# Theta's weights cast on their way in, angles rounded to int32, and v of batch 1 held behind them

## The chip, the cores and the metric

The kernel runs on one core of one Trainium2 chip. The metric is the device time of one execution in microseconds; before the change its median over three runs is 208.49 us (208.44 to 208.51). The engines are called PE (TensorE), DVE (VectorE), ACT (ScalarE), POOL (GpSimd) and SP (SyncE, which here only issues transfers). Transfers are issued by SP and ACT (hardware queues, q1 and q10 in the profile) and by POOL (the software queue, q0), and all of them are carried by the same 16 DMA engines. Only transfers issued on POOL change the type on the way.

## The reference

q, k and v have 8 batches, 8 heads, 576 positions of 64 numbers. First comes a linear attention without a softmax, with its rows normalised; then a block that mixes tokens with a phase.

```
kv  = einsum('bhsd,bhse->bhde', k, v)
out = einsum('bhsd,bhde->bhse', q, kv)
x   = out / sqrt(mean(out*out, -1) + 1e-6) * g_norm        # then heads side by side: [8, 576, 512]
theta = x @ w_theta                                        # [512, 512]
y   = w_tok_r @ (x * cos(theta)) + w_tok_i @ (x * sin(theta))   # per batch, [576, 576]
u   = x + y
result = u + relu(u @ w_ch)                                # w_ch [512, 512]
```

## The kernel before

A batch is worked as 576 = 4 x 128 + 64 rows: four full row tiles (j = 0 to 3) and a tail of 64 rows (names that end in e). For each of the 8 batches TensorE forms k'v, turns q, multiplies it with k'v (raw), and the rows are normalised: ACT squares, DVE sums, a root (ACT for batch 0, POOL for the others), DVE scales to x in fp16. x is turned (by TensorE for the first four batches, by a transposing transfer later), scaled by g on ACT or DVE into xT, and multiplied with theta's weights `wth` (task th, line 451). The angle is then brought into one turn: ACT takes the whole turns (pt, line 467), DVE subtracts them (ar, line 472), an absolute value for the cosine (ab), ACT evaluates sine and cosine (lines 490 and 497), and DVE multiplies x with both (z). TensorE mixes tokens (y, line 543) with the turned token weights wT, DVE makes u, TensorE multiplies with `wch` (v in the trace's line 451), and DVE finishes.

How whole turns are taken: theta's weights are scaled by 1/TURN as they are cast to fp16, TURN being an eighth of a turn, so that the product comes in eighths; adding `MAGIC`, 1.5 * 2^23 * 8, in fp32 leaves only whole multiples of 8 eighths; DVE subtracts MAGIC again and then the angle, which leaves minus the rest.

Theta's weights come in on SP's queue as fp32, into memory that z of batch 1 uses later (`wth_s`, the tile zm1 in the trace), and four instructions scale and cast them (`scale_theta`, lines 241 and 245: three on ACT and one on DVE). z of batch 1 therefore depends on these four.

The order of the work is a list written out by hand: the program makes tasks with their dependencies, numbered as they are made, and `TURNS` names the numbers in the order in which they are issued (a star picks the second of two engines, r9 issues nine idle products). Each engine works its own instructions in that order and waits on semaphores for the others; nothing is reordered on the chip.

Three places of the start matter here. POOL's queue first issues q of batch 0, then a copy of one number of v's tails of batch 0 ("hold p", line 232), which waits until that transfer has landed; behind it stand the two token weights (w_tok_i, then w_tok_r: wn for 512 rows, wnt for the last 64), then a copy of one number of v of batch 1 ("hold v"), and behind that q of batches 1 and 2 and the channel weights. SP issues k of batch 0 and v's tails, g, theta's weights, v of batch 1 and k of batch 1, then k and v of later batches, whose buffers have to come free first. ACT's queue issues v's heads of batch 0. TensorE turns the token weights as tasks wt (lines 639 and 640), the first two of them between the first and the second theta product.

Of the kernel before, what the change touches and what calls it, by code (L numbers as in the profile page):

```python
# [9 lines left out]
FP32 = mybir.dt.float32  # L10
# [22 lines left out]
3 4 0 1 2 5 6 7 9 8 32 33 44 r1 52 38 18 19 20 21 22 11 10 13 25 26 23 24 27 29 210 31 30 45* 60 61*  # L33
34 35 39 40 41 36* 37 42* 43* 76 46 77* 53* 47 48 62 78 54 68 28 63 12 64 79 49 69 80 50 65 66 55
15* 16* r9 51 67 70 14 56 17* 71 87 85 88 102 57 81 86* 72 73 103 138 142 139 143 82 83 74 58 59 75
95 93 94* 96 89 90* 130 91 104 92* 97 109 123 84 106 105 131* 98 134 140 116 135* 99 141* 107 124
125 108 132 100 117 110 133* 101 111 118 112 146 136 127 126* 137 172 176 144 164 213 214 215 216
113 128 114 147 120 119* 121 145 129 115 122 177 165 219 220* 217 218 173 233 166 226 221 222 234*
168 178 235 174 167 357 206 208 207 209 223 175 179 391 236 224 237 392 169 148 160 170 156 240 227
377 149 157 225 171 228 241* 238 229 239 158 159 230 150 152 247 242 161 378 248 243 254 153 154 190  # L40
162 255 244 231 245 264 256 265 191* 155 151 163 232 384 192 266 246 249 257 385 197 370 258 271 193
371* 259* 180 181* 278 260 185 250 268 267* 269 272 251 252 364 365 366 367 279 273 280 281 270 261*
253 186 282 274* 285 187 262 275 276 286 195 368* 369* 372 386 287 188 263 292 200 202 373 361 212
211 362 363 512 359 360 358 194 532 521 515 516 517 518 374 375 387 196 293 201 277 294 388 198 283
288* 376 284 203 389 295* 296 289 519 297 182 379 390 327 315 407 393 328 380 520 199 543 508 509
510 511 290 183 408 381 319 320 316 405 394 298 291 422 398 317 321 329 395 382 396 383 406 423 399
318 322 330 397 307 400 303 401 402 415 424 403 416 417 522 308 523 404 524 525 411 409 410 323 309
310 299 533 413 534 419 418 425* 426 427 420 414 304 412* 535 536 300 324 305 306 526 311 312 325
# [51 lines left out]
def kernel(  # L100
# [24 lines left out]

    eps = 1e-6

    UNIT = 8.0
    MAGIC = 1.5 * 2.0 ** 23 * UNIT
    TURN = 2.0 * math.pi / UNIT  # L130
    SHRINK = 1.0 - 1e-6
# [765 lines left out]
    with tc.manual_schedule():  # L897
# [7 lines left out]
        for i in range(NKV):  # L905
            clear_tails(i)
# [31 lines left out]
```

## Time and profile before

| what | value |
|---|---|
| median of the runs | 208.49 us |
| the profiled execution, its span | 208.02 us, 206.0 us |
| TensorE, VectorE, ScalarE, GpSimd busy | 187.4, 172.7, 138.9, 85.8 us |
| granted TensorE clock | 1.000 |
| DMA engines | 43.67 MB, mean 212 GB/s |
| casts of theta's weights on ACT and DVE | 3 x 619 ns, 1 x 417 ns |
| whole turns on ACT, 512 columns | 32 x 596 ns |
| subtraction on DVE, 512 columns | 32 x 681 ns |

Times inside the profile count from the span's start. The span is from the first to the last instruction; the execution's own time is 2.0 us longer. A row of a timeline gives start, duration, engine, line, instruction and, in brackets, the idle time of the engine just before it and what ended it. A row of a transfer gives size and the time from its issue to its landing. The page shows the DMA engines busy by nine tenths or more in all but one of the first 32 of 40 slices, so transfers stand in each other's way over most of the run.

### The profile page before, as it was taken

Reading aid. Unit: us, or ns where it says so; the run is one execution under the profiler, and the core shown is the slowest. Engines: PE = TensorE matmul, PEld = TensorE weight load, DVE = VectorE, ACT = ScalarE, POOL = GpSimd, SP = SyncE. Lnnn points to the kernel's source line nnn. Section 1 sums busy time; section 2 is a strip of 40 time slices with the busy share of each in tenths; the row PEclk is TensorE's granted clock in tenths of the full one; section 3 lists DMA queues with packets and bytes.
Section 4 is the critical chain, followed back from the end, with each engine's and each line's share of the span. In section 5 each row is a group of like instructions: output and inputs, shape, how many; then the busy total and the mean of one; then the engine's idle time right before and its main releaser. Section 6 shows DMA issues by size and latency. Waiting matters only on the chain.

```text
span 206.0 us, 5268 instructions
## 1 busy us (share of the span) xinstructions
PE 187.4 (91%) x2078; PEld 132.3 (64%) x2078; DVE 172.7 (84%) x362; ACT 138.9 (67%) x275; POOL 85.8 (42%) x90
## 2 busy tenths in 40 slices
PE   0378799999999999999999999997989999999992
PEld 0355468895786777576776767665856746756671
DVE  6039896789999999999898999996989999689572
ACT  2018799758799588987896678666936983976101
POOL 7030061263965565884608381283629420101300
PEclk9999999999999999999999999999999999999999
DMA  6999999999999899999999999999999552644144
GB/s 197 269 269 303 231 244 189 276 354 265 231 178 186 243 277 212 293 261 170 223 233 190 302 231 130 225 219 309 282 158 238 132 101 79 179 127 153 45 123 153
DMA packets 74952, 43.67 MB, mean 212 GB/s; under 512 B 44577, under 2 KB 70497, under 8 KB 74929
## 3 DMA queue, kind: packets, MB, share of 16 engines
q1 hardware_dynamic: 59216, 33.17, 67.7%
q0 software_dynamic: 14512, 9.00, 28.6%
q10 hardware_dynamic: 1200, 1.18, 1.7%
q8 instruction: 16, 0.26, 0.5%
q14 instruction: 8, 0.06, 0.1%
HBM read 33.06 MB, written 9.44 MB: 206 GB/s over the span
## 4 chain that ended last, share of the span: by engine, by line
PE 59%; DMA 15%; ACT 11%; DVE 10%; issue 2%; SPq 1%; DVEq 0%; POOL 0%; ACTq 0%
PE y L543 28%; PE th L451 10%; PE v L451 9%; DMA vt<-in_v_dram 5%; DMA wnt<-in_moe_w_tok_i_dram 4%; DMA qD<-qh 4%; DVE arg L472 2%; PE raw L323 2%; DMA uD<-wn 2%; ACT kbd L286 2%; ACT sc L497 2%; ACT sc L490 1%; DVE zm L520 1%; ACT arg L480 1%; PE wps L639 1%
## 5 line engine op out<-in xcount | busy, mean ns | idle before, releaser
L364 POOL TENSOR_TENSOR rt<-ss,mhalf 128x8 f32<-128x8 f32 (+1 forms) x35 | 54.6, 1563 | 66.3 <-DVE ss L354 66.0
L543 PE MATMUL y<-wT,zm 128*128 128x320 f16 (+1 forms) x512 | 76.8, 286 | 0.8 <-DVE ot L585 0.6
L543 PEld LDWEIGHTS <-zm 128*128 128x128 f16 x512 | 48.1, 98 | 15.8 <-issue 1.3
L548 DVE SCALAR_TENSOR_TENSOR wn<-y,gcol,xT 128x320 f16<-128x320 f32 (+1 forms) x64 | 30.9, 510 | 6.6 <-PE y L543 6.3
L451 PE MATMUL th<-wth,xT 128*128 128x512 f16 x128 | 32.1, 379 | 1.3 <-ACT xT L419 1.0
L467 ACT ACTIVATE arg<-th 128x512 f32<-128x512 f32 (+1 forms) x40 | 21.8, 554 | 14.4 <-PE th L451 13.9
L451 PE MATMUL v<-wch,wn 128*128 128x512 f16 x124 | 30.7, 380 | 0.0
L266 PE MATMUL kv<-vt,kt 128*64 128x64 f32 x640 | 21.6, 228 | 8.6 <-DMA vt<-in_v_dram 8.6
L345 ACT ACTIVATE sqb<-raw 128x512 f32<-128x512 f32 x32 | 18.8, 594 | 14.5 <-PE raw L323 14.5
L497 ACT ACTIVATE sc<-arg,quarter 128x512 f16<-128x512 f32 (+1 forms) x40 | 26.6, 675 | 0.3
L266 PEld LDWEIGHTS kv<-vt,kt 128*64 128x64 f32 x640 | 20.6, 143 | 9.5 <-issue 9.2
L472 DVE SCALAR_TENSOR_TENSOR arg<-arg,th 128x512 f32<-128x512 f32 (+1 forms) x40 | 24.9, 628 | 1.9 <-ACT arg L467 1.5
L490 ACT ACTIVATE sc<-arg 128x512 f16<-128x512 f32 (+1 forms) x40 | 22.7, 583 | 3.2 <-DVE arg L472 2.7
L354 DVE TENSOR_REDUCE ss<-sqb 128x8 f32<-128x520 f32 x32 | 22.0, 687 | 3.3 <-ACT sqb L345 3.3
L520 DVE TENSOR_TENSOR zm<-x,sc 128x1024 f16<-128x1024 f16 x32 | 21.8, 685 | 1.8 <-ACT sc L497 1.5
L386 DVE TENSOR_TENSOR x<-raw,rt 128x512 f16<-128x512 f32 x32 | 21.7, 684 | 0.8 <-POOL rt L364 0.5
L451 PEld LDWEIGHTS <-xT 128*128 128x128 f16 x128 | 11.6, 98 | 11.4 <-ACT xT L419 1.4
L451 PEld LDWEIGHTS <-wn 128*128 128x128 f16 x124 | 11.5, 98 | 10.7 <-issue 0.4
L480 ACT ACTIVATE arg<-arg 128x512 f32<-128x512 f32 (+1 forms) x31 | 17.5, 575 | 1.2 <-DVE arg L472 1.1
L543 PE MATMUL y<-wT,zt 128*128 128x320 f16 (+1 forms) x64 | 18.3, 286 | 0.0
L286 ACT CAST kbd<-kv 64x256 f16<-64x256 f32 (+1 forms) x24 | 8.5, 355 | 12.9 <-PE kv L266 12.6
L286 ACT COPY us<-ups 128x512 f16<-128x512 f16 (+1 forms) x17 | 8.5, 497 | 12.6 <-PE ups L281 11.5
(82 smaller groups left out, 229.7 us busy)
## 6 DMA issues: line engine op xcount, KB each, us to landing
vt<-in_v_dram SPq DMA_DIRECT2D x7, 1024.0 KB, 10.1
kt<-in_k_dram SPq DMA_DIRECT2D x7, 1024.0 KB, 8.2
out_dram<-ot SPq DMA_DIRECT2D x24, 256.0 KB, 2.7
qh<-in_q_dram POOLq DMA_DIRECT2D x7, 512.0 KB, 8.0
out_dram<-ot POOLq DMA_DIRECT2D x7, 256.0 KB, 3.6
kt<-in_k_dram SPq DMA_DIRECT2D x2, 512.0 KB, 4.6
vt<-in_v_dram ACTq DMA_DIRECT2D x2, 512.0 KB, 8.5
kt<-in_k_dram SPq DMA_DIRECT2D x8, 128.0 KB, 7.8
```

What stands on the lines that cost most here:

```text
L266: nc.tensor.matmul(t[i * D:(i + 1) * D, hp - lo, :], ks, vs, start=(hp == lo and j == 0), stop=(hp == lo + n - 1 and j == NT - 1),)
L354: nc.vector.reduce_sum(out=ss[:], in_=sq_sb.pop((b, j))[:], axis=AXX)
L364: nc.gpsimd.tensor_tensor(out=rt[:], in0=ss[:], in1=mhalf[:, 0:h], op=ALU.pow)
L386: nc.vector.tensor_tensor(out=x_pair[b, p][:, :, a * HC:(a + 1) * HC].rearrange("p t (h e) -> p h t e", e=D), in0=r[:].rearrange("p (h t e ...
L451: nc.tensor.matmul(t[:], piece(kc), w[:, kc, :], start=first, stop=last)
L467: nc.scalar.activation(out=arg[:, 1, :], in_=th_ps[b, j][:], func=AFT.Copy, bias=MAGIC)
L472: nc.vector.scalar_tensor_tensor(out=arg[:, 0, :], in0=arg[:, 1, :], scalar=MAGIC, in1=th_ps.pop((b, j))[:], op0=ALU.subtract, op1=ALU.sub ...
L490: nc.scalar.activation(out=sc[:, 0, :], in_=arg_sb[b, j][:, 0, :], func=AFT.Sin, bias=0.0, scale=-TURN * SHRINK,)
L497: nc.scalar.activation(out=sc_sb[b, j][:, 1, :], in_=arg_sb.pop((b, j))[:, 1, :], func=AFT.Sin, bias=quarter[:], scale=-TURN * SHRINK,)
L520: nc.vector.tensor_tensor(out=dst, in0=x.unsqueeze(1).broadcast_to((P, 2, w)), in1=sc[:], op=ALU.mult)
L543: nc.tensor.matmul(t[:, 0:hi - lo], s, wT[:, w, lo:hi], start=n == 0, stop=n == len(z) - 1)
L548: nc.vector.scalar_tensor_tensor(out=uTb[b % NUT][:, c, lo:hi], in0=y_ps.pop((b, h, c))[:, 0:hi - lo], scalar=gcol[:, 0:1], in1=xTb[b % NX ...
```

## The change

Five edits go together.

- Theta's weights are issued on POOL's queue and land in `wth` as fp16, unscaled. The four scalings and `wth_s` are gone, and z of batch 1 no longer waits for them.
- The whole turns are made by ACT as the angle times 1/TURN, TURN now being a whole turn, written as int32, the conversion rounding to a whole number. DVE reads the angle from PSUM, multiplies it with 1/TURN and subtracts that int32. The rest has the other sign than before, and so has the scale of the sine.
- A new task "hold w" on POOL adds one number of v's buffer of batch 1 and one of `wth`. It waits until theta's weights have landed.
- The load of v of batch 1 waits for "hold w" (it writes the number that "hold w" reads). So it starts only after theta has landed.
- One number of that buffer is set to zero by DVE at the start, so that "hold w" reads something defined.

In `TURNS` the four scalings, the old load of theta and the new tasks shift all numbers by three; apart from the removed and the added tasks the order is the same. The load of theta stands behind q of batch 0, "hold w" behind the token weights.

```
     def theta_in():
-        nc.sync.dma_start(out=wth_s, in_=moe_w_theta.rearrange("(kc p) c -> p kc c", p=P))
+        nc.gpsimd.dma_start(out=wth[:], in_=moe_w_theta.rearrange("(kc p) c -> p kc c", p=P))
...
+    def hold_both(a, b):
+        nc.gpsimd.tensor_tensor(out=gate[:], in0=a, in1=b, op=ALU.add)
...
-    def scale_theta(kc, eng):
-        if eng == "ACT":
-            nc.scalar.activation(
-                out=wth[:, kc, :], in_=wth_s[:, kc, :], func=AFT.Copy, scale=1.0 / TURN
-            )
-        else:
-            nc.vector.tensor_scalar(
-                out=wth[:, kc, :], in0=wth_s[:, kc, :], scalar1=1.0 / TURN, scalar2=None,
-                op0=ALU.mult,
-            )
...
     def whole_turns(b, j):
...
-        nc.scalar.activation(out=arg[:, 1, :], in_=th_ps[b, j][:], func=AFT.Copy, bias=MAGIC)
+        nc.scalar.activation(
+            out=arg[:, 1, :].bitcast(I32), in_=th_ps[b, j][:], func=AFT.Copy, scale=1.0 / TURN
+        )
...
     def reduce_arg(b, j):
         nc.vector.scalar_tensor_tensor(
-            out=arg[:, 0, :], in0=arg[:, 1, :], scalar=MAGIC,
-            in1=th_ps.pop((b, j))[:], op0=ALU.subtract, op1=ALU.subtract,
+            out=arg[:, 0, :], in0=th_ps.pop((b, j))[:], scalar=1.0 / TURN,
+            in1=arg[:, 1, :].bitcast(I32), op0=ALU.mult, op1=ALU.subtract,
         )
...
-            bias=0.0, scale=-TURN * SHRINK,
+            bias=0.0, scale=TURN * SHRINK,
...
-    wth_in = add("load wth", "SP", theta_in)
-    got["wth"] = [add(f"wg {kc}", "DVE|ACT", lambda e, kc=kc: scale_theta(kc, e), [wth_in])
-                  for kc in range(NKC)]
+    got["wth"] = [add("load wth", "POOL", theta_in)]
...
+    ahead = add("hold w", "POOL", lambda: hold_both(vt[1][0:1, 0:1], wth[0:1, 0, 0:1]), got["wth"])
...
-                       lambda t=t, src=src: heads_in(nc.sync, t, src, b, all8), old),
+                       lambda t=t, src=src: heads_in(nc.sync, t, src, b, all8),
+                       [*old, *([ahead] if t is vt[1] and b == 1 else [])]),
...
-                    [co, *of("y", b - NZ), *(got["wth"] if b == 1 else [])],
+                    [co, *of("y", b - NZ)],
...
+        nc.vector.memset(vt[1][0:1, 0:1], 0.0)
```

The first place where the order shows it is POOL's queue at the start (wth is theta's weights, wn and wnt the token weights, vt_66 and vt_67 v of batches 0 and 1, qh and qe the rows and tails of q; in brackets the semaphores waited for). Before:

```order
L209 DMA qe_71<-in_q_dram 64x4x64 x2
L232 COPY gate<-vt_66 1x1 [waits DMAHW5_49]
L215 DMA wn_86<-in_moe_w_tok_i_dram 128x2304
L220 DMA wnt_88<-in_moe_w_tok_i_dram 64x576
L215 DMA wn_85<-in_moe_w_tok_r_dram 128x2304
L220 DMA wnt_87<-in_moe_w_tok_r_dram 64x576
L232 COPY gate<-vt_67 1x1 [waits DMAHW1_49,Pool_49]
L203 DMA qh_69<-in_q_dram 128x8x256 [waits DMASW0_49]
```

and now:

```order
L206 DMA qe_71<-in_q_dram 64x4x64 x2
L220 DMA wth<-in_moe_w_theta_dram 128x4x512
L232 COPY gate<-vt_66 1x1 [waits DMAHW5_49]
L212 DMA wn_86<-in_moe_w_tok_i_dram 128x2304
L217 DMA wnt_88<-in_moe_w_tok_i_dram 64x576
L212 DMA wn_85<-in_moe_w_tok_r_dram 128x2304
L217 DMA wnt_87<-in_moe_w_tok_r_dram 64x576 [waits DMASW0_49]
L229 TENSOR_TENSOR gate<-vt_67,wth 1x1 [waits DMASW4_49,DVE_49,Pool_49]
L232 COPY gate<-vt_67 1x1 [waits DMAHW0_49,Pool_49]
L200 DMA qh_69<-in_q_dram 128x8x256 [waits DMASW1_49]
```

Theta's load stands ahead of the first gate and of the token weights, and the new gate stands behind the token weights and ahead of the old gate on v of batch 1.

The second place is SP's queue at the start (kt is k, gcol is g, zm_77 the memory in which theta's weights landed). Before:

```order
L193 DMA vt_66<-in_v_dram 64x8x64
L229 DMA gcol<-in_g_norm_dram 64x1 x2
L223 DMA zm_77<-in_moe_w_theta_dram 128x4x512 [waits DMAHW0_49]
L187 DMA vt_67<-in_v_dram 128x8x256 [waits DMAHW1_49]
L193 DMA vt_67<-in_v_dram 64x8x64 [waits DMAHW2_49]
L187 DMA kt_65<-in_k_dram 128x8x256 [waits DMAHW3_49]
```

and now:

```order
L190 DMA vt_66<-in_v_dram 64x8x64
L226 DMA gcol<-in_g_norm_dram 64x1 x2
L184 DMA vt_67<-in_v_dram 128x8x256 [waits DMAHW0_49,Pool_49]
L190 DMA vt_67<-in_v_dram 64x8x64 [waits DMAHW1_49]
L184 DMA kt_65<-in_k_dram 128x8x256 [waits DMAHW2_49]
```

Theta's load is gone from SP, and the load of v of batch 1, with its tails and k of batch 1 behind it, waits for POOL's gate.

The third place is ScalarE's part of batch 0 (sqb the squares, wth<-zm the scalings, xT the scaled turned x, rs the roots, arg the whole turns). Before:

```order
L345 ACTIVATE sqb_94<-raw 128x8x64
L241 ACTIVATE wth<-zm_77 128x512 x3
L345 ACTIVATE sqb_95<-raw 128x8x64
L419 ACTIVATE xT_82<-xps,gcol 128x4x128
L373 ACTIVATE rs<-ss 128x8
```

and now:

```order
L334 ACTIVATE sqb_94<-raw 128x8x64
L334 ACTIVATE sqb_95<-raw 128x8x64
L408 ACTIVATE xT_82<-xps,gcol 128x4x128
L362 ACTIVATE rs<-ss 128x8
L362 ACTIVATE rs<-ss 128x4
```

The three scalings between the two squares are gone; the rest of ScalarE's order is the same. On VectorE the one scaling goes likewise, behind the first two x.

More of the change, by code (lines that the diff above doesn't have):

```diff
@@ L126 @@
     eps = 1e-6
[L128 to L130 removed]
+    TURN = 2.0 * math.pi
     SHRINK = 1.0 - 1e-6
```

101 lines of the change are left out of this document (50 added, 51 removed).

## The prediction

> **What bounds the kernel now.** I read the page's totals first, then the chain of waits, then the first 37 us engine by engine, because every edit but one acts there.
>
> ```profile
> span 206.0 us, 5268 instructions
> PE 187.4 (91%) x2078; PEld 132.3 (64%) x2078; DVE 172.7 (84%) x362; ACT 138.9 (67%) x275; POOL 85.8 (42%) x90
> PE y L543 28%; PE th L451 10%; PE v L451 9%; DMA vt<-in_v_dram 5%; DMA wnt<-in_moe_w_tok_i_dram 4%; DMA qD<-qh 4%; DVE arg L472 2%; PE raw L323 2%; DMA uD<-wn 2%; ACT kbd L286 2%; ACT sc L497 2%; ACT sc L490 1%; DVE zm L520 1%; ACT arg L480 1%; PE wps L639 1%
> ```
>
> TensorE is busy 187.4 of 206.0 us, and the third row, the chain of waits by line, has most of its weight there too, with two transfers of the start behind it (v and the tail of w_tok_i). A change of the start is therefore worth what it moves TensorE's first full stretch, if no transfer is due in the meantime. The chain in order of time (start, duration, what), with TensorE's first products ahead of it:
>
> ```profile
> 8.57 1.98 PE L266 MATMUL kv<-vt,kt 128*64 128x64 f32 x32 [8.57 <-DMA vt<-in_v_dram]
> 2.59 10.96 DMA vt<-in_v_dram
> 14.27 8.78 DMA wnt<-in_moe_w_tok_i_dram
> 23.10 0.22 PE wps L640
> 23.81 0.97 PE th L451 x4
> ```
>
> TensorE's idle time is 18.6 us in all, and 8.57 of it are this first wait. The tails of v of batch 0 land at 13.55, POOL's gate opens, the token weights are issued, the tail of w_tok_i lands at 23.05, TensorE turns it and goes on to the second theta product. But a second path ends almost at the same place, and it is the one that the change touches. The timelines of TensorE and ScalarE (start, duration, instruction, idle before it and what ended it):
>
> ```profile
> 19.65 0.38 PE L323 MATMUL raw<-kbd,qT 128*128 128x128 f16 x4 [0.26 <-DVE x L386]
> 21.77 1.04 PE L451 MATMUL th<-wth,xT 128*128 128x512 f16 x4 [1.00 <-ACT xT L419]
> 23.75 1.04 PE L451 MATMUL th<-wth,xT 128*128 128x512 f16 x4
> 18.99 1.66 ACT L241 ACTIVATE wth<-zm 128x512 f16<-128x512 f32 x3
> 20.55 0.58 ACT L345 ACTIVATE sqb<-raw 128x512 f32<-128x512 f32 x1
> 21.02 0.69 ACT L419 ACTIVATE xT<-xps,gcol 128x512 f16<-128x512 f16 x1
> 24.82 0.60 ACT L467 ACTIVATE arg<-th 128x512 f32<-128x512 f32 x1 [0.29 <-PE th L451]
> 25.43 1.28 ACT L377 ACT_TABLE_LOAD   x1
> ```
>
> The first theta product waits 1.00 us for ScalarE's xT, which stands behind three scalings of theta's weights and a square. The second must be over before ScalarE's arg of 24.82 and the table load behind it.
>
> **The change, part by part.**
>
> *The scalings go.* ScalarE's three take 20.55 - 18.99 = 1.56 us of its queue. Not all of it comes back: the square behind them needs the raw product that TensorE ends at 20.03, so it starts at about 20.08 instead of 20.55, and xT at 20.57 instead of 21.02. The gain at the first theta product is 0.45 us (21.32). VectorE's one scaling frees room too:
>
> ```profile
> 20.11 0.42 DVE L245 TENSOR_SCALAR wth<-zm 128x512 f16<-128x512 f32 x1
> ```
>
> Behind it stands VectorE's xT for the second theta product, which moves up by as much as it can and was ahead of need before. The two theta products start 23.75 - 21.77 = 1.98 us apart, and between them stand two turns of w_tok_i, of which the first waits for the landing of 23.05, some 0.1 us. If w_tok_i is there by 22.2 (rows) and 22.5 (tail), the second product starts at 23.2 instead of 23.75: 0.55 us. From there all three engines run the same order as before, TensorE nearly without a gap, and the 0.55 us stand.
>
> *Theta's weights move from SP's queue to POOL's.* They are issued behind q of batch 0, about 4.5 instead of 4.82 us.
>
> ```profile
> 3.17 1.27 POOL L209 DMA_DIRECT2D qe<-in_q_dram  x2
> zm<-in_moe_w_theta_dram SPq DMA_DIRECT2D x1, 1024.0 KB, 11.9
> qe<-in_q_dram POOLq DMA_DIRECT2D x2, 32.0 KB, 11.4
> wn<-in_moe_w_tok_i_dram POOLq DMA_DIRECT2D x1, 576.0 KB, 8.7
> ```
>
> Before, theta lands at 4.82 + 11.9 = 16.7, and the second of q's two last parts near 15.7. Now theta follows q in the same queue. The nearest transfer of its kind is the channel weights, same shape and cast; in the stretch 37 to 38 us, when they are most of the queue's work, it moved 0.21 MB in 1 us, so 0.52 MB take 2.5 us. The queue of k and v is then empty, since v of batch 1 is held, so q should end near 14 to 15 and theta near 16.5 to 17.5. It is due at 21.3: the wait costs nothing.
>
> *The token weights stand behind theta.* They are issued at 13.7 as before. The views of the DMA queues (packets, MB, share of the 16 engines) for 0 to 14 and 14 to 17.2 us, then both queues for 18 to 24, then 37 to 38:
>
> ```profile
> q1 hardware_dynamic: 2426, 1.63, 46.2%
> q1 hardware_dynamic: 830, 1.20, 102.4%
> q0 software_dynamic: 315, 1.08, 89.7%
> q1 hardware_dynamic: 310, 0.32, 18.7%
> q0 software_dynamic: 229, 0.21, 127.7%
> ```
>
> In 14 to 17.2 k's and v's queue (q1) carries theta's rest and the head of v; w_tok_i then flows at 0.18 MB/us against v. Its 0.66 MB take 3.7 us at that pace, so starting at 16.5 to 17.5 it ends at 20.2 to 21.2, ahead of 22.5. w_tok_r follows, ahead of its old time. No loss.
>
> The Trainium skill, "DMA: Bandwidth & Descriptors", section "Queues, rings and completion order", says that an engine takes turns between queues packet by packet. The 315 against 310 packets agree. By that rule theta in POOL's queue could take turns with the tails of k and v, which it stood behind before, and push the landing of 13.55 out; only q in front of it prevents that.
>
> *v of batch 1 is held.* The gate "hold w" needs theta, and stands on POOL behind the four token issues.
>
> The rows of both queues stand with the change above: theta went in on POOL ahead of the first gate, a gate on theta ahead of the one on v, and on SP the load of v of batch 1 now waits for POOL. Behind it on SP stand v's tails and all of k of batch 1; the next on SP are k and v of later batches at 35.65, behind a wait for TensorE's products. On POOL stand "hold v", q of batches 1 and 2 and the channel weights. What they had:
>
> ```profile
> 6.51 1.82 SPq L187 DMA_DIRECT2D vt<-in_v_dram  x1
> vt<-in_v_dram SPq DMA_DIRECT2D x1, 1024.0 KB, 20.7
> 35.65 0.99 SPq L187 DMA_DIRECT2D kt<-in_k_dram  x2
> 27.77 1.97 POOL L203 DMA_DIRECT2D qh<-in_q_dram  x2
> qh<-in_q_dram POOLq DMA_DIRECT2D x1, 512.0 KB, 8.0
> 36.48 0.39 PE L281 MATMUL qps<-ident,qh 128*128 128x128 f16 x4
> vt<-in_v_dram SPq DMA_DIRECT2D x1, 128.0 KB, 8.2
> 52.38 0.74 PE L266 MATMUL kv<-vt,kt 128*64 128x64 f32 x17
> 55.18 1.04 PE L451 MATMUL th<-wth,xT 128*128 128x512 f16 x4 [0.25 <-DVE xT L421]
> ```
>
> v is issued at about 17 instead of 6.5, but its first bytes moved only once theta was through. Of the 1.20 MB in 14 to 17.2, theta's rest is about 0.73 (by 14 us q1 had moved 1.63 MB, 0.32 beyond k and the tails of v), so v loses a head start of about 0.47 MB, or 1.2 us of the engines. In return the token weights flow unopposed in that time, and leave v the engines 2 us earlier. The work is the same; if the engines stay busy, v lands near 27.2 again, and q of batch 1 at 27.77 + 8.0 = 35.8. TensorE asks for it at 36.48 - 0.55 = 35.93: just in time. The tails of v of batch 2 (this view's 8.2 us belong to the issue at 44.19) land at 52.4 and are needed eight products after 52.38, now after 51.83: a stall of 0.3 us, of which the 0.25 us that TensorE waited at 55.18 swallow nearly all.
>
> *The rounding.* ScalarE writes int32 with a scale instead of fp32 with a bias, VectorE reads PSUM first and int32 second, 40 times each.
>
> ```profile
> L472 DVE SCALAR_TENSOR_TENSOR arg<-arg,th 128x512 f32<-128x512 f32 x32 | 21.7, 681 | 1.9 <-ACT arg L467 1.5
> L585 DVE SCALAR_TENSOR_TENSOR ot<-v,us 128x512 f32<-128x512 f32 x15 | 10.2, 683 | 0.3
> L467 ACT ACTIVATE arg<-th 128x512 f32<-128x512 f32 x32 | 18.9, 596 | 14.4 <-PE th L451 13.9
> L497 ACT ACTIVATE sc<-arg,quarter 128x512 f16<-128x512 f32 x32 | 22.7, 718 | 0.3
> ```
>
> PSUM as first operand costs 683 against 681 ns. No row has an int32 conversion. Bounds: nothing below (no row of these forms is faster by more than noise), and above the 122 ns by which the dearest activation exceeds this one; VectorE's has 2% of the chain, some 4 us or six instructions, and ScalarE's fewer, so up to 1 us for both. I take 0, from the row of the same operation.
>
> **Sum:** -0.55 at the start, and 0.1 taken off for transfers that are due later and do not move: -0.45. The profiled execution took 208.02 us (206.0 and 2.0 around it), 0.47 under the median of 208.49; its sum is 207.57, and the same difference from the median gives **208.05 us**.
>
> **Rivals.**
>
> *The held v comes late (slower).* Place: "hold v" and the q behind it. If the token weights do not start until 17.5, as before, the engines idle for the 1.2 us that v had. v lands at 28.4, q of batch 1 at 37.0 against 35.93: 1.0 us of stall against 0.55 of gain; the v tails of batch 2 land at 53.6, 0.95 late on the old plan, of which 0.25 are swallowed. One stretch gives some of it back, 30 to 31 us, in which the transfers kept the 16 engines 0.68 busy (the last two numbers: DMA share, GB/s):
>
> ```profile
> 30.00:31.00 1.00, 1.00 (x12) 0.74 (x13) 1.00 (x4) 1.00 (x4) 1.00 (x3) 1.00 0.68 82
> ```
>
> That is 0.3 us. The end is 0.4 to 0.7 later: 209.0. It decides from a delay of v of about 0.6 us. For it: the token weights issued at 13.7 moved nothing up to 17. Against it: the queue ahead of them was then full, and now is not. The Trainium skill, "SBUF — State Buffer", section "SBUF: two separate sides", says that some VectorE operations keep GpSimd from writing the descriptors of its DMAs, and that SP's queue is free of this; by that rule the token weights, issued on POOL while VectorE works, could start late whatever stands ahead of them, which is this rival at 209.0; the trace shows the late start, not its cause.
>
> *The start gains, and it is gone later (no change).* q of batch 1, with 0.15 us to spare, or some later transfer holds TensorE on the old time: 208.4.
>
> *The conversion is dearer than the forms next to it (slower or same).* 0.5 us of the 1 against the gain: 208.55.
>
> *More than the start's 0.55.* If the raw product did not hold the square, 1.56 us would come back: 207.0. The 0.26 us of TensorE's own wait at 19.65 speaks against it.
>
> **How the numbers follow.** Forecast 0.44, late v 0.25, gone later 0.20, conversion 0.06, more 0.05. About 0.2% (0.42 us) is what a measurement tells from no change. The forecast's own range, 207.8 to 208.25, straddles it: 0.32 of its chance count as faster, 0.12 as the same. Of the late v 0.16 pass the bound and 0.09 do not, of the conversion half. Faster 0.32 + 0.05 = 0.37; slower 0.16 + 0.03 = 0.19; the same 0.12 + 0.09 + 0.20 + 0.03 = 0.44. The range reaches from 207.6 to 209.1, so that it takes in the price of the late v.
>
> **What would show it.** Right: no scaling rows; ScalarE's xT near 20.6, the first theta product near 21.3, the second near 23.2; w_tok_i's tail before 22.5; v of batch 1 at 27 to 27.5 and no wait for q at 36; L467's and L472's rows at 596 and 681 ns. Wrong: a wait of TensorE for wth or wnt in the twenties, for qh near 36 or for vt near 52, or VectorE's row above 700 ns.

## The result, and the profile after

The changed kernel takes 207.05 us (median of 7 runs, 206.56 to 207.78) against 208.49 us for the kernel before in the same series; the ratio is 0.9927, 95% interval 0.9906 to 0.9947. That is 1.44 us less, about three times the 0.45 forecast and below the forecast range. Two later series (e4 and e15 below) gave 0.9945 (0.9915 to 0.9976) and 0.9924 (0.9897 to 0.9951), or 1.19 and 1.41 us between the medians. Ratios and intervals leave out executions more than 1.5% above the fastest of the same kernel; medians and ranges are over all executions. The profiled execution took 206.56 us. Single executions of either kernel spread by a microsecond or more, so the terms below are read from profiles, stage by stage, and only their sum from times.

The page of the changed kernel, its first rows:

```profile
span 204.6 us, 5267 instructions
PE 188.3 (92%) x2078; PEld 132.8 (65%) x2078; DVE 172.5 (84%) x362; ACT 137.6 (67%) x272; POOL 86.4 (42%) x92
```

ScalarE has three instructions fewer, GpSimd two more. The timelines of TensorE and ScalarE at the start (start, duration, instruction, idle before it and what ended it), then GpSimd's gate for theta and the two landings that mattered (size, time from issue):

```profile
17.79 2.11 PE L640 MATMUL idle<-fill,ident 128*128 128x512 f16 x9
21.53 1.04 PE L440 MATMUL th<-wth,xT 128*128 128x512 f16 x4 [0.60 <-ACT xT L408]
22.73 0.22 PE L631 MATMUL wps<-ident,wnt 64*128 64x64 f16 x1
23.37 1.04 PE L440 MATMUL th<-wth,xT 128*128 128x512 f16 x4
20.30 0.60 ACT L334 ACTIVATE sqb<-raw 128x512 f32<-128x512 f32 x1 [1.04 <-PE raw L312]
20.80 0.68 ACT L408 ACTIVATE xT<-xps,gcol 128x512 f16<-128x512 f16 x1
17.02 0.18 POOL L229 TENSOR_TENSOR gate<-vt,wth 1x1 f32<-1x1 f32 x1 [0.78 <-DVE qT L277]
wnt<-in_moe_w_tok_i_dram POOLq DMA_DIRECT2D x1, 72.0 KB, 6.2
vt<-in_v_dram SPq DMA_DIRECT2D x1, 1024.0 KB, 9.8
```

ScalarE now waits for the raw product and works xT at once; TensorE waits 0.60 us for it instead of 1.00. Theta's gate is passed at 17.0, w_tok_i's tail needs 6.2 us instead of 8.8 and lands near 20.8, two microseconds before TensorE turns it; v of batch 1, issued at 17.2, lands at 27.0. The whole turns and their subtraction, from the groups of instructions of the changed kernel:

```profile
L456 ACT ACTIVATE arg<-th 128x512 int32<-128x512 f32 x32 | 18.9, 597 | 14.1 <-PE th L440 13.7
L463 DVE SCALAR_TENSOR_TENSOR arg<-th,arg 128x512 f32<-128x512 f32 x32 | 21.8, 685 | 1.9 <-ACT arg L456 1.5
```

That is 597 against 596 ns, and 685 against 681.

Set instruction against instruction, TensorE in the changed kernel is 0.37 us ahead of its old time from 23 us on and stays so to 139 us: no wait for q at 36, none for v's tails at 52. Then come two more steps. At 140 us the transposed q of batch 6 is waited for; this row of TensorE's timeline is from before, the next from after:

```profile
140.62 0.40 PE L323 MATMUL raw<-kbd,qD 128*128 128x128 f16 x4 [1.46 <-DMA qD<-qh]
```

```profile
139.70 0.40 PE L312 MATMUL raw<-kbd,qD 128*128 128x128 f16 x4 [0.89 <-DVE x L375]
```

The wait is 0.57 us shorter (in the second row q has landed and VectorE's x ends the wait), and nearly all of that stays to TensorE's end, 1.00 us ahead. And the span ends 1.4 us earlier: behind the last store, which ScalarE issues (rows of before and after), the old kernel has 206.0 - 202.5 = 3.5 us, the new one 204.6 - 201.5 = 3.1.

```profile
202.51 0.37 ACTq L613 DMA_DIRECT2D out_dram<-ot  x1
```

```profile
201.51 0.36 ACTq L604 DMA_DIRECT2D out_dram<-ot  x1
```

So in this pair the start gives 0.37, the wait at 140 us 0.6 and the end 0.4. Which of them belong to the change was the question.

### The profile page after: what moved, and what is told of

Its sections match the earlier page's. It is cut to its first block, busy times and chain, and to the rows that moved or that the text cites. A ratio compares the mean times of both kernels' runs of the same rounds, so it can differ in the third digit from the quotient of the medians.

```text
span 204.6 us, 5267 instructions
## 1 busy us (share of the span) xinstructions
PE 188.3 (92%) x2078; PEld 132.8 (65%) x2078; DVE 172.5 (84%) x362; ACT 137.6 (67%) x272; POOL 86.4 (42%) x92
## 4 chain that ended last, share of the span: by engine, by line
PE 67%; ACT 12%; DVE 8%; DMA 7%; issue 2%; POOL 1%; DVEq 0%; ACTq 0%; POOLq 0%
PE y L534 29%; PE th L440 11%; PE v L440 11%; DMA vt<-in_v_dram 5%; PE kv L255 3%; PE raw L312 3%; DMA uD<-wn 2%; DVE arg L463 2%; ACT kbd L275 2%; ACT sc L488 2%; PE wps L630 2%; ACT sc L481 1%; ACT arg L471 1%; ACT xT L408 1%; PE qps L270 1%
## 5 line engine op out<-in xcount | busy, mean ns | idle before, releaser
L456 ACT ACTIVATE arg<-th 128x512 int32<-128x512 f32 (+1 forms) x40 | 21.8, 554 | 14.1 <-PE th L440 13.7
L334 ACT ACTIVATE sqb<-raw 128x512 f32<-128x512 f32 x32 | 18.9, 595 | 14.4 <-PE raw L312 14.3
L488 ACT ACTIVATE sc<-arg,quarter 128x512 f16<-128x512 f32 (+1 forms) x40 | 26.6, 675 | 0.3
L463 DVE SCALAR_TENSOR_TENSOR arg<-th,arg 128x512 f32<-128x512 f32 (+1 forms) x40 | 25.0, 632 | 1.9 <-ACT arg L456 1.5
L471 ACT ACTIVATE arg<-arg 128x512 f32<-128x512 f32 (+1 forms) x31 | 17.5, 575 | 1.2 <-DVE arg L463 1.1
```

What stands on the lines that cost most here:

```text
L456: nc.scalar.activation(out=arg[:, 1, :].bitcast(I32), in_=th_ps[b, j][:], func=AFT.Copy, scale=1.0 / TURN)
L463: nc.vector.scalar_tensor_tensor(out=arg[:, 0, :], in0=th_ps.pop((b, j))[:], scalar=1.0 / TURN, in1=arg[:, 1, :].bitcast(I32), op0=ALU.mul ...
L488: nc.scalar.activation(out=sc_sb[b, j][:, 1, :], in_=arg_sb.pop((b, j))[:, 1, :], func=AFT.Sin, bias=quarter[:], scale=-TURN * SHRINK,)
```

## Experiments

**The rounding alone**, in the kernel before (e1), and **the scalings alone taken out** (e2).

```
 e1  -  ACT: arg = th + MAGIC (fp32)      +  ACT: arg = int32(th / 8)
     -  DVE: (arg - MAGIC) - th           +  DVE: th / 8 - arg
 e2      def scale_theta(kc, eng):
     +      return
     ...
     +  nc.vector.memset(wth[:], 0.0)
```

> The kernel before with the rounding alone: theta's weights still scaled by 8/(2*pi) after landing, ScalarE writes the whole turns as int32 with scale 1/8, VectorE multiplies PSUM by 1/8 and subtracts the int32. Everything else as before. Theory A (the rounding costs and saves nothing; it all comes from the start): 208.49 within 0.2 us; the 40 + 40 instructions keep their means of 596 and 681 ns; TensorE's instructions stand where they stood, no shift above 0.1 us, and the transposes of uD around 122 to 127 us again take some 5.1 us on SP. Theory B (the rounding feeds the later gain, for instance through VectorE reading SBUF second): TensorE's shift grows in steps along the batches and the time falls by 0.3 us or more. A second use: if SP's 2.5 us issue at 123 us is an accident of one profiled execution, it is gone here though nothing ahead of it moved.

> The kernel before without the four scalings: the weights that the theta product reads are set to zero once at the start and theta's own load goes on as before, on SP and into the same scratch, and is not used, so the angles come out as zero and the output is another one. Loads, queues and the hold are those of before; only the start of ScalarE and VectorE is relieved. Theory A (the start alone does it, and what comes later, at 122 to 140 us, follows from everything standing earlier): first theta product about 0.4 us earlier, the later gain at 140 us too, time 207.1 to 207.4. Theory B (the later gain belongs to the moved loads of the start): the first theta products 0.2 to 0.45 us earlier, that shift constant to the end, time 208.0 to 208.2. Theory C (the tail of w_tok_i, which lands at 23.05 with the old loads, holds the second theta product whatever ScalarE does): shift at most 0.1 us from 23 us on, time 208.4 to 208.5.

e1: 208.82 us, ratio 1.0015 (0.9989 to 1.0042). By the time the rounding costs between -0.2 and 0.9 us; its groups keep their times to within 3 ns per instruction:

```profile
L467 ACT ACTIVATE arg<-th 128x512 int32<-128x512 f32 x32 | 18.9, 596 | 14.3 <-PE th L451 13.9
L474 DVE SCALAR_TENSOR_TENSOR arg<-th,arg 128x512 f32<-128x512 f32 x32 | 21.8, 684 | 1.9 <-ACT arg L467 1.5
```

The wait at 140 us was 0.82 us here, with nothing changed ahead of it. Over the profiles that leave SP's order and TensorE's start alone it is 0.79 to 1.52 us with the old loads and 0.58 to 1.45 with the new: it varies from execution to execution, and the 0.57 us of the first pair are not shown to be a gain of the change.

e2: 209.22 us, ratio 1.002 (0.9986 to 1.0054). TensorE's timeline shows why nothing came of it:

```profile
17.56 2.10 PE L650 MATMUL idle<-fill,ident 128*128 128x512 f16 x9
23.32 0.22 PE L641 MATMUL wps<-ident,wnt 64*128 64x64 f16 x1 [0.24 <-DMA wnt<-in_moe_w_tok_i_dram]
23.97 1.04 PE L452 MATMUL th<-wth,xT 128*128 128x512 f16 x4
```

ScalarE is free, and w_tok_i's tail lands at 23.3: theory C. The nine idle products give a measure for the rest: they start 2.41 to 2.45 us behind the end of batch 0's k'v in every profile, however late k and v come, and the second theta product follows 6.41 us after their start here.

**The hold taken out** of the changed kernel (e3), **the scalings put back** into it (e7), and **the hold alone** in the kernel before (e9).

```
 e3  -  ahead = add("hold w", "POOL", lambda: hold_both(...), got["wth"])
     +  ahead = add("hold w", "POOL", lambda: None)
     -  nc.vector.memset(vt[1][0:1, 0:1], 0.0)
 e7  +  ACT x3, DVE x1:  wth[:, kc, :] = 1.0 * wth[:, kc, :]     (old places in TURNS)
 e9  +  POOL, behind the token weights:  gate = vt[1][0, 0] + wth_s[0, 0, 0]
     +  nc.vector.memset(vt[1][0:1, 0:1], 0.0)
     (load of v of batch 1 moved behind it)
```

> The changed kernel without the hold: v of batch 1 is issued on SP near 6.5 us as before and waits for nothing, the gate on theta is gone from GpSimd; theta still lands cast through GpSimd's queue, unscaled. Prediction's reading (v takes turns with the token weights, and w_tok_i lands late): w_tok_i's tail lands at 22.5 to 23.5 us, the second theta product 0.1 to 0.5 us later than with the hold, time 207.1 to 207.5. If the later gain at 140 us hangs on when v and q of batch 1 land: TensorE's shift against the kernel before stays at the start's -0.1 to -0.4 and does not grow at 140 us, time 208.1 to 208.4. If the hold is worth nothing: 207.0 within 0.15.

> The changed kernel with four scalings by 1.0 put back at their old places in the orders of ScalarE (three) and VectorE (one), in place on theta's weights; loads, hold and rounding stay changed. If the relief of ScalarE is what the start gains (the prediction's step): the first theta product 0.2 to 0.45 us later than in the changed kernel, near 21.75 to 22.0 us, the second near 23.7 to 23.9, time 207.4 to 207.8. If the moved loads are what the start gains, because w_tok_i no longer comes at 23 us or later: th second product within 0.1 us of 23.36, time as the changed kernel's. The end stays at 3.9 us either way.

> The kernel before with the hold alone: GpSimd's gate on theta's landing (theta still on SP, fp32, scaled) stands behind the four token issues, and v of batch 1 waits for it; scalings, rounding and the 113 DMAs of SP and ScalarE as before. If the moved loads are worth something only together with the relief of ScalarE (the reading so far: w_tok_i and ScalarE's queue end together): w_tok_i's tail lands at 20 to 22 us, the first theta product stays at its time behind the scalings, the end of the span stays 4.3 us behind the last product, time 208.2 to 208.7. If the hold by itself carries most of the gain: second theta product near 23.4 us and time at or below 207.9. If v of batch 1, held, comes late without the cast load: wait for q near 36 us, time above 208.8.

e3: 209.32 us, ratio 1.0008 (0.9976 to 1.0040). The row of the wait that came:

```profile
23.99 0.41 PE L630 MATMUL wps<-ident,wn 128*128 128x128 f16 x4 [1.34 <-DMA wn<-in_moe_w_tok_i_dram]
```

v of batch 1, issued early, runs beside w_tok_i, which takes 9.9 us; the second theta product comes 7.30 us after the idle products. The mechanism was expected, at less than a third of its size (0.1 to 0.5 us, against 7.30 - 5.58 = 1.7, of which the wait is about 1.5), and with a time of 207.1 to 207.5 us. Behind the wait comes something that was not expected, the second theta product at half the pace:

```profile
25.16 1.89 PE L440 MATMUL th<-wth,xT 128*128 128x512 f16 x4
```

It takes 1.89 us instead of 1.04. The granted clock is 0.50 for 3.41 us from 24.6 us on in this profile, and batch 1 comes another 1.1 us late (10.5 us behind this product instead of 9.4). Over e3's executions, the seven with a granted clock of 0.996 or more take 207.43 to 209.39 us (median 208.07), the five below it 209.34 to 214.25. So without the hold no gain is left in the time, but how much of that is the wait and how much the clock was not separated.

e7: 208.23 us, 0.9979 (0.9962 to 0.9996). e9: 209.17 us, 1.0013 (0.9982 to 1.0043). Both lie above the times expected (207.4 to 207.8, 208.2 to 208.7); of the gain e7 keeps 0.44 us, about as much as the end's term below. Their TensorE rows, e7 first:

```profile
18.14 2.11 PE L651 MATMUL idle<-fill,ident 128*128 128x512 f16 x9
22.29 1.04 PE L451 MATMUL th<-wth,xT 128*128 128x512 f16 x4 [1.00 <-ACT xT L419]
24.14 1.04 PE L451 MATMUL th<-wth,xT 128*128 128x512 f16 x4
```

```profile
17.83 2.11 PE L657 MATMUL idle<-fill,ident 128*128 128x512 f16 x9
22.09 1.04 PE L459 MATMUL th<-wth,xT 128*128 128x512 f16 x4 [1.01 <-ACT xT L427]
23.93 1.04 PE L459 MATMUL th<-wth,xT 128*128 128x512 f16 x4
```

In both w_tok_i is early (5.5 to 6.4 us from issue) and ScalarE's scalings hold the product with the old wait of 1.0 us. From the idle products to the second theta product it is 6.00 and 6.10 us. With the same measure the changed kernel has 23.37 - 17.79 = 5.58, and 5.58 to 5.59 in each of its other profiles with the hold; the kernel before has 5.99 in e1 and e6, and 23.75 - 17.29 = 6.46 in its own profile. The 0.40 us between 5.99 and 5.59 lie ahead of the first theta product: that is ScalarE's relief.

The further 0.47 us of the kernel before have two parts. Only 0.14 lie between the two theta products (1.98 us apart there; 1.84 in the changed kernel, e1 and e6), where w_tok_i is waited for. The other 0.33 come from q's tails of batch 0, which TensorE turns ahead of the raw products (before, then after):

```profile
15.85 0.27 PE L281 MATMUL qps<-ident,qe 128*128 128x128 f16 x2 [1.01 <-DVE kbd L288]
```

```profile
15.29 0.28 PE L270 MATMUL qps<-ident,qe 128*128 128x128 f16 x2
```

The second part of these tails lands at 15.71 before and at 14.54 after. (The row of before names VectorE for the wait; but there and in e2, e6, e9, e11 and e14 TensorE starts 0.13 to 0.14 us behind this landing.) With theta on SP it lands at 15.7 to 16.4 us, with theta on GpSimd and the hold at 14.4 to 14.7, with theta on GpSimd and no hold (e3) at 15.3. Where batch 0's k'v ends early (14.84 in before, 15.11 in e2), the late tails push VectorE's first x, and the raw product behind it, back by 0.33 us against the idle products (x starts 1.62 us after their start instead of 1.29); where it ends later, by 0.11 (e9) or not at all (e1, e6).

So ScalarE's relief is worth 0.40 us at the same start, and the moved loads up to 0.47 us on top when k'v ends early. Neither shows in a time without the other.

**The end's list.** At the end SP waits for eight semaphores, DMAHW0 to DMAHW7, which the transfers of SP and ScalarE take in turn. The moments at which SP passed these waits, from the trace (the first is another wait):

```
before  202.61 | 204.66 204.73 204.79 204.85 204.91 204.97 205.03 205.09
after   201.61 | 201.67 201.73 201.80 201.86 201.92 202.81 203.34 203.66
```

Before, the last store holds the first wait, and seven that are long fulfilled follow at 0.06 us each. After, it holds the last. The two queues issued 113 transfers before (113 = 14 x 8 + 1) and 112 after, because theta's moved to GpSimd. To test it, one late store changes its queue, in the changed kernel to SP (e5: 113), in the kernel before to GpSimd (e6: 112):

```
 e5  TURNS:  - 1043*   + 1043
 e6  TURNS:  - 1040    + 1040*
```

> The changed kernel with one late store (half of batch 6's second row block group, issued by GpSimd near 190 us) moved to SP's queue, which is idle there; nothing else. Theory L (the list of waits at the end): the program ends with SP waiting, one after another, for eight DMA semaphores that the DMAs of SP and ScalarE take in turn; before there were 113 of them and the last store had the first place in the list, so seven waits of 0.06 us stood behind its landing, after there were 112 and it has the last place. With 113 again the time from the start of TensorE's last product to the end of the span is 4.3 us instead of 3.9, and the time 0.4 us above the changed kernel's, in 207.4 to 208.1. Theory S (the shorter end belongs to the changed transfers or is scatter): that time stays at 3.9 us, and the kernel's time with it.

> The kernel before with one late store (batch 6, first rows, issued by SP near 190 us) moved to GpSimd's queue, so that SP and ScalarE issue 112 DMAs. Theory L (the list of waits at the end): the time from the start of TensorE's last product to the end of the span is 3.9 us instead of 4.3, and the time 0.4 us below the kernel before, ratio 0.998; nothing before 180 us moves. Theory S: 4.3 us, ratio 1.000.

The last store and the span of e5, then of e6:

```profile
202.50 0.37 ACTq L604 DMA_DIRECT2D out_dram<-ot  x1
span 206.0 us, 5267 instructions
```

```profile
203.11 0.36 ACTq L613 DMA_DIRECT2D out_dram<-ot  x1
span 206.2 us, 5268 instructions
```

3.5 us in e5 (the changed kernel with 113 transfers), 3.1 in e6 (the one before with 112): the end has swapped with the count, theory L. In time e6 is 0.50 us below the kernel before (0.9977, 0.9949 to 1.0005, an interval that still holds no change), e5 0.99 us below it (0.9942, 0.9909 to 0.9975): that is what the change brings without the end's term. All other profiles fit: 3.5 with 113 transfers, 3.1 with 112.

**What comes between the second theta product and 31 us.** From that product to the first k'v product of batch 1, near 33 us, the changed kernel takes 9.41 to 9.42 us in all profiles (first pair, e4, e5, e15, and e8, e10 and e12 below), the kernels with the old loads 9.42 (before, and e11 below), 9.63 (e1), 9.78 (e6) and 9.83 (e2). Rows of e6, VectorE's two sign-bit instructions, GpSimd's issues of q, and TensorE:

```profile
27.44 0.79 DVE L482 TENSOR_SCALAR arg<-arg 128x512 int32<-128x512 int32 x1
28.51 0.64 DVE L482 TENSOR_SCALAR arg<-arg 128x512 int32<-128x512 int32 x1
27.08 1.83 POOL L203 DMA_DIRECT2D qh<-in_q_dram  x2 [0.29 <-issue]
28.64 0.38 PE L639 MATMUL wps<-ident,wn 128*128 128x128 f16 x4 [0.32 <-DVE wT L288]
```

These instructions take 0.42 us elsewhere. In the changed kernel's profile they come earlier (26.87 and 27.57) and q is issued later (27.59): TensorE is ahead, and v, held, opens the gate at 27.1 to 28.0 us against 26.6 to 27.3 in before, e1, e2 and e6 (27.8 in e11). It is a matter of timing and no safety of the changed kernel: e7, whose scalings put VectorE later, has one such instruction at 0.83 us and takes 9.51. Two kernels set the collision up and take it apart:

```
 e13  -  "hold v" waits for v of batch 1 (27.1 us)   +  for the first reduced angle (26.1 us)
 e14  +  five copies of one number on POOL between "hold v" and the issue of q
```

> The changed kernel with GpSimd's gate ahead of q of batches 1 and 2 on VectorE's first reduced angle of batch 0 instead of on the landing of v of batch 1, so that these four transfers are issued from about 26.4 us, across VectorE's two sign-bit instructions near 26.9 and 27.6 us. Theory: GpSimd, while it issues a transfer, slows that kind of VectorE instruction; both take 0.6 to 0.85 us instead of 0.42, TensorE waits 0.2 to 0.4 us for VectorE's wT near 28 us, and the second stretch (second theta product to the one near 55 us) is 0.2 to 0.4 us longer than the 31.42 to 31.43 us of the changed kernel. Against it: the instructions keep 0.42 us, and the slow ones so far came from something else that stands close to the issues. Time 207.2 to 208.0 by the theory, 207.0 to 207.6 against it.

> The kernel before with five copies of one number on GpSimd between the landing of v of batch 1 and the issue of q, so that q is issued about 0.9 us later, near 28.0 to 28.6 us. By the theory of the collision the two sign-bit instructions near 27.5 and 28.2 us take 0.42 us (one of them may still be hit), TensorE does not wait near 28.7 us, and the stretch from the second theta product to the one near 55 us is 31.4 us where it was 31.6 to 31.8 in three of four profiles of kernels with the old loads. Q of batch 1 then lands near 36.5 us and may hold TensorE by up to 0.5 us, which the same stretch would show behind 36 us. Time 208.2 to 208.8.

e13, then e14:

```profile
26.90 0.80 DVE L473 TENSOR_SCALAR arg<-arg 128x512 int32<-128x512 int32 x1
27.98 0.64 DVE L473 TENSOR_SCALAR arg<-arg 128x512 int32<-128x512 int32 x1
26.54 1.82 POOL L200 DMA_DIRECT2D qh<-in_q_dram  x2 [0.29 <-issue]
28.11 0.38 PE L630 MATMUL wps<-ident,wn 128*128 128x128 f16 x4 [0.33 <-DVE wT L277]
```

```profile
27.89 0.42 DVE L487 TENSOR_SCALAR arg<-arg 128x512 int32<-128x512 int32 x1
28.59 0.42 DVE L487 TENSOR_SCALAR arg<-arg 128x512 int32<-128x512 int32 x1
29.34 1.82 POOL L203 DMA_DIRECT2D qh<-in_q_dram  x2
```

Made and unmade as expected: e13 takes 9.78 us to batch 1 and 31.79 to the product near 55 us, e14 9.42 and 31.47, with no wait for q at 36 us. In e14 the third such instruction, at 32.82 us, now falls on GpSimd's issue of the channel weights and takes 0.59 us. The times, 207.35 (0.9933, 0.9905 to 0.9960) and 208.55 us (1.0012, 0.9985 to 1.0040), are too coarse to show 0.36 us.

**The changed kernel again**, twice, for its size.

> The changed kernel once more, for a second profile and a second interval. If the step of -0.6 us at 122 to 140 us and the -0.4 us at the end belong to the kernel, TensorE's shift against the kernel before is again -0.37 up to 140 us and about -1.0 behind it, and the ratio is 0.993 within 0.0015. If they belong to one execution, the step is missing from this profile or from the shifts that the other profiles of this call show, and the ratio comes nearer 0.997.

> The changed kernel a third time beside the kernel before, for its size: by the terms found so far (ScalarE's relief 0.40 us, the end's list 0.43 us, the collision near 27 us 0.2 to 0.4 us when it strikes, the token weights 0 to 0.46 us) the difference of the medians is -1.0 to -1.6 us; the second theta product 5.59 us behind the start of the nine idle products, the end 3.9 us behind the start of the last product.

The ratios are 0.9945 (e4, between the two that were set against each other) and 0.9924 (e15, 1.41 us between the medians). The step at 140 us is missing from e4 (its wait is 1.45 us), the end's is there; TensorE ends 0.44 us ahead of the first profile of before. e15 has 5.59 us from the idle products to the second theta product, and the end at 3.9 us behind TensorE's last product.

**Tries at a faster version**, of the changed kernel except e11. Idle products while TensorE waits for k and v (e10, and e11 in the kernel before), and the transposed q of batch 6 issued earlier on SP (e8, e12).

```
 e10, e11  TURNS:  + r20 ahead of the first product
 e8   TURNS:  - 952 917 352* 826 941 919      + 941 952 352* 826 917 919
 e12  TURNS:  - 952 917 352* 826 941 919      + 917 941 952 352* 826 919
 (917: load of k of batch 7, 941: q of batch 6, 952: its tails, 826: x's tails)
```

> The changed kernel with 20 idle products on TensorE ahead of its first one, in the 8.5 us in which it waits for k and v of batch 0; nothing reads them. In all profiles so far the fp32 products of the start go from 53 to 29 ns apart at one moment, which lies between 12.6 and 16.3 us from execution to execution (12.6 in the kernel before, 14.3 in the changed one). If that pace is set by how long TensorE has been busy: the first 32 products take 1.15 us instead of 1.98, the raw products and the first theta product come 0.4 to 0.9 us earlier than 21.5, time 206.3 to 206.9, and the runs scatter less. If the moment does not depend on it: the profile as the changed kernel's, 207.0 to 207.6.

> The kernel before with the same 20 idle products ahead of TensorE's first one. With the pace of the start made equal in both kernels, their difference is the change's own: by the reading so far 0.5 us at the start, 0.43 us at the end, and up to 0.4 us where VectorE's sign bits fall on GpSimd's issues of q near 27 to 28 us. In the kernel before w_tok_i's tail lands at 23.05 us whatever TensorE does, so an earlier pace is worth 0 to 0.2 us here: 208.2 to 208.6, 1.3 to 2 us above the changed kernel with the same products. If the scatter of the start alone made the two kernels differ, they now differ by the end's 0.43 us only.

> The changed kernel with two moves in SP's order near 128 to 133 us: the transposing load of q of batch 6, second half, goes ahead of the one of q's tails and of x's tails of batch 5, and the load of k of batch 7 goes behind the latter. In every profile so far TensorE waits 0.8 to 1.5 us near 140 us for that transfer, which SP issues at 132 to 133 us. If SP's queue alone sets that wait: it is issued near 129 us, the wait falls below 0.3 us, and the time by 0.6 to 1.3 us against the changed kernel, unless the wait of 0.5 to 0.9 us near 152 us for z grows in its place. If the transposes share one limit whatever their order, the wait stays, or moves to q's tails or x's tails near 144 us, and the time is the changed kernel's.

> The changed kernel with the transposing load of q of batch 6, second half, moved in SP's order ahead of those of q's tails and x's tails near 129 us, and the load of k of batch 7 left just ahead of it (where the earlier try put that load behind, TensorE's wait moved from 140 us to k and v of the next batch at 145 and 147 us, 0.9 and 1.0 us). If the wait at 140 us is only SP's order: it falls from 0.9 to 1.5 us to below 0.4, none comes at 145 us, and the time goes 0.4 to 0.9 us below the changed kernel's (207.0 to 207.6 so far), 206.3 to 207.0. If the gain is taken by the next wait, that for z near 152 us: it grows from 0.5 to above 1.0 us and the time stays.

The pace did rise: e10's first 32 products take 1.15 us instead of 1.98.

```profile
8.53 1.15 PE L255 MATMUL kv<-vt,kt 128*64 128x64 f32 x32 [0.82 <-DMA vt<-in_v_dram]
```

The times did not follow: medians of 210.35 and 210.09 us with wide scatter, ratios 0.9939 (0.9886 to 0.9993) and 1.0003 (0.9955 to 1.0052): the miss of the study. The granted clock over the span is 0.992 or less in 7 of e10's and 8 of e11's 12 executions, against 4 of 29 of the kernel before beside them. In e11's profile it falls to 0.50 for 3.41 us at 13.9 us, and the k'v products of 14.2 us are back at the slow pace. e10's profile is 0.3 us ahead of the changed kernel's first one up to 129 us and loses some 4 us around 140 us, most of it in one wait:

```profile
142.34 0.61 PE L312 MATMUL raw<-kbd,qD 128*128 128x128 f16 x4 [3.58 <-DMA qD<-qh]
```

The transposed q lands 2.6 us later there than in the changed kernel (142.29 against 139.65), and the clock is at 0.50 from 141.6 us on, again for 3.41 us. Whether the idle products bring on either was not tested.

e8 (207.63 us, 0.9916, 0.9881 to 0.9952) removes the wait at 140 us and, in its profiled execution of 209.02 us, gets two others:

```profile
145.29 0.69 PE L255 MATMUL kv<-vt,kt 128*64 128x64 f32 x16 [0.88 <-DMA vt<-in_v_dram]
146.94 2.08 PE L255 MATMUL kv<-vt,kt 128*64 128x64 f32 x64 [0.96 <-DMA vt<-in_v_dram]
```

e12 (208.03 us, 0.9973, 0.9941 to 1.0005) avoids these and keeps the first, longer:

```profile
140.67 0.40 PE L312 MATMUL raw<-kbd,qD 128*128 128x128 f16 x4 [1.94 <-DMA qD<-qh]
```

Issued 2.2 us earlier but behind the load of k, q's transfer lands at 140.62 us, no earlier than the 139.65 of the changed kernel; ahead of that load, in e8, it lands 3.3 us after its issue. What holds it up behind k was not tested. No version here is shown to beat the changed kernel.

## Why the prediction was wrong, point by point

*What bounds.* Right, with both paths named: ScalarE's scalings and w_tok_i's landing end almost together. e2 (1.002) and e9 (1.0013) show that removing one alone brings nothing that their times can tell.

*The scalings go.* Mechanism right, size close: 0.45 forecast for the first theta product, 0.40 measured at equal start. The first pair shows only 0.24 (21.53 against 21.77), because k and v landed half a microsecond later in that execution of the changed kernel (9.11 against 8.57). But the forecast held the raw product fixed, ending at 20.03; at the same start it comes 0.33 us earlier once q's tails are early. The forecast had these tails right (q done at 14 to 15, measured 14.5) and did not follow them to the products that wait for them.

*Theta on GpSimd's queue.* Right: 16.5 to 17.5 forecast, landed at 16.85, gate passed at 17.02.

*The token weights.* Right: 20.2 to 21.2 forecast, near 20.8 measured. The 0.55 us for the second product measures 0.40 for ScalarE and 0.14 for w_tok_i in the forecast's own profile, so these two were priced rightly; with q's 0.33 the gain at the same start is 0.87 us there, and 0.40 where k'v ends later (e1, e6).

*v held.* Right: 27.2 forecast, 27.0 measured, no wait for q at 36 us; the stall at v's tails of batch 2 is absent in the first profile and 0.31 us in e15, of which only 0.10 is won back by 55 us (forecast: nearly all).

*The rounding.* Right, 0.

*The sum* is the step that failed. It stopped at the second theta product and let "the 0.55 us stand" to the end, with 0.1 us taken off for transfers. Three terms were missing, put at nothing without a reason. The raw product behind q's tails: 0 to 0.33 us. The end: 0.43 us, because a transfer fewer on SP and ScalarE changes the place of the last store in the final list of waits; this is systematic, and the program alone would have told it (113 transfers and eight semaphores). And the stretch behind the second theta product, 0 to 0.41 us, where the old timing lets VectorE and GpSimd collide. The 0.1 us taken off was fair: 0 in the first profile, 0.21 in e15. The terms as measured, then: 0.40 + 0.43 = 0.83 us always, up to 0.47 us from the moved loads (0.33 q's tails, 0.14 w_tok_i) and up to 0.41 from the collision, less up to 0.21 for v's tails, by execution. That bounds the gain between 0.62 and 1.71 us, and the differences of the medians, 1.19 to 1.44 us, lie inside. How often each varying term strikes was not counted, so the sum is bounded and not closed.

*The profile taken for the median.* The old kernel's profile was one with q's late tails and without the collision (9.42 us). So a gain that three of the other four profiles with the old loads offered (e1, e2 and e6, not e11) could not be read from it.

*The rivals.* The held v did not come late; nothing was lost at 36 us; the conversion cost nothing. "More than the start's 0.55" named 207.0, the right time for a wrong reason: the square still waits for the raw product (1.04 us idle at 20.30), and ScalarE's 1.56 us did not come back.

## What to carry to other kernels

Where two paths end together, cost an edit by the pair, and take the gain from the distance to a fixed event ahead of both, not from times since the start. When a transfer lands earlier, follow it to everything that waits for it, and not only to the product in view. Count the transfers per queue before and after: a change that moves one can shift the place of the last store in the final list of waits, here by seven steps of 0.06 us. And read more than one execution of the kernel before: what is a narrow fit in the one profiled is a loss in others.

## What the runs showed of the hardware that was not expected

*GpSimd's issue slows VectorE.* Over the first fourteen profiles, of 80 sign-bit instructions of 512 columns that overlap no issue by GpSimd none took above 0.43 us. Of 32 that overlap one, the 22 that started 0.32 to 0.57 us after the issue did took 0.58 to 0.84 (14 of them stand at 53 to 56 us, one in each profile, with the old loads and the new). The other ten, which started before the issue, in its first 0.28 us or in its last 0.06, kept 0.41 to 0.42. The Trainium skill, "SBUF — State Buffer", section "SBUF: two separate sides", says that GpSimd and certain VectorE operations share one pair of ports as an exclusive lock, where the later one waits. The rows agree with it; the prediction had weighed that rule only in the other direction, GpSimd kept waiting.

*TensorE's pace in the start.* The same 32 products of batch 0 (rows of the changed kernel and of e5, whose start is the same program):

```profile
14.21 1.15 PE L255 MATMUL kv<-vt,kt 128*64 128x64 f32 x32
```

```profile
13.96 1.98 PE L255 MATMUL kv<-vt,kt 128*64 128x64 f32 x32
```

Both have the column of the granted clock at 1.00, but the trace's record of the clock begins only at 14.06 us in the changed kernel and at 16.05 in e5, so ahead of that the column measures nothing. The pace goes from 1.98 to 1.15 us for 32 products at about the moment at which the record begins: between 12.5 and 17.1 us in the profiles without idle products ahead, 3.5 to 8.5 us behind the first product. In the changed kernel the raw products start between 15.4 and 16.2 us with it. The Trainium skill, "TensorE: Matmul & The Clock Gate", section "What's actually happening", lets the clock double after a busy window of about 3.4 us that runs freely and does not start with the kernel. The moments do not contradict that, though they spread over 5 us (TensorE has gaps here), and e10, busy from 1.5 us on, was at the fast pace by 8.5.

*The clock falls back after some waits.* In the three profiles with a mean clock below 0.995 (e3, e10, e11) the record shows 0.50 for 3.41 us, once each ahead of the program's end, after waits of TensorE of 1.3 us (e3), 3.6 us (e10) and 1.5 and 0.8 us (e11). Waits of 1.4 to 1.9 us at 140 us in before, e4, e12 and e14 were followed by no such fall, so the length of the wait alone does not decide it; what does was not tested.
